# Five score banks for part of the scores, products cut in two, and a new written order, in clustered attention followed by a SoLU block

## The chip, the cores and the metric

The kernel runs on one core of one Trainium2 chip. The metric is the device time of one execution in microseconds (us). Matmuls run on TensorE (PE in the profile; PEld is its weight load), element-wise work on VectorE (DVE), ScalarE (ACT) and GpSimd (POOL); SyncE (SP) issues nearly all DMAs.

## The reference, cut to what matters

Clustered attention, then a SoLU feed-forward block with a layer norm. With B = 4, H = 8, S = 768, D = 64 and 16 clusters:

```
q_assign = argmax over c of <q_n, c_n>        # the same for k_assign
mask     = q_assign[:, :, :, None] == k_assign[:, :, None, :]
scores   = where(mask, q k^T / sqrt(D), -1e9)
x        = softmax(scores) @ v                # heads side by side: 3072 tokens x 512
h        = x @ w_in                           # 512 -> 1024
solu     = h * softmax(h)
out      = layernorm(solu) * g_ln @ w_out     # 1024 -> 512
```

## The kernel before, in words

*The attention.* Work goes by 16 pairs of heads (batch b, pair p). For each pair q and k are loaded (`ld`), turned so that features lie on partitions (batch 0: on TensorE through the region `hreg`, `tp`, and copied out, `xa`, L405; the others: on VectorE, `xt`, L419), multiplied by the centroids on TensorE (`cl`, L450, into the bank `csc`), turned back (`tb`, L471), reduced to a maximum per token (`mx`, L484), compared with it (`oh`, L489) and turned again (`ot`, L495). q and k are cast to bf16 into the tile `qk` (`ca`, L443 to L447) and the one-hot rows are placed beneath them (`pl`, L507, L512 or L514), with a zero fill (`bl`, L523), so that one matmul gives score plus cluster match. v is loaded (`lv`) and cast (`cv`, L532).

*Scores.* 294 score banks follow one another: 24 of 384 columns (the first pair), then 270 of 512. `S` (L593) writes a bank on TensorE, `E` (L599) is its exponential on ScalarE, `V` (L616) multiplies it by the values, `N` (L628, L641) divides a group of heads by its row sums on VectorE into x. Groups are numbered in order; groups 0 and 1 belong to the first pair, and a unit of the later ones has three banks. The scores take turns in a ring of three PSUM banks (`ps_s`); three more banks are `hreg`, one holds the values' sums (`ps_o`), one is shared by `cl`, y and small turns (`ps_m`).

*The feed-forward part.* It goes by 24 blocks f of 128 tokens. x is transposed by DMA, for two blocks at a time in the first three batches (`tx`, L671; the last block on TensorE); `h` (L702, four parts of two matmuls) fills two of hreg's three banks, even blocks the banks 0 and 1, odd ones 1 and 2; `hm` (L708) is the maximum, `ex` (L714) the exponential, `u` (L721) the product; u is transposed (`tu`, L726 by DMA; the last two blocks on TensorE, `ptu`); `bn` and `ag` (L732, L736) are the statistics, `at` and `al` (L742 to L751) the scale on GpSimd; `y` (L768, four parts) multiplies by w_out; `sc` (L786 or L788) scales, `ou` stores. w_out is prepared first: eight sums weighted by g (`su`, L568, L571), their mean over rows by a matmul (`me`, L576, into bank 2 of hreg), and eight centred rows (`ce`, L579).

*What sets the order.* Every step is registered by `add` with its engine, a cost, the steps that it needs, and others that it comes after. The tables `ORDER` list for each engine the kinds of steps in the order in which that engine issues them, written out by hand or by a planner outside of the program; the n-th step of a kind that was registered for an engine is the n-th of that kind in the table. `AWAY` gives single steps to another engine than their own. Each engine works through its queue in order, and waits where an operand or a bank isn't ready. `uses` (L230) tells which banks of `hreg` an instruction touches, so that those of other banks don't wait for it.

Of the kernel before, what the change touches and what calls it, by code (L numbers as in the profile page):

```python
# [10 lines left out]
F32 = mybir.dt.float32  # L11
# [11 lines left out]
class Weave:  # L23
# [6 lines left out]
        ld4 lv si ld3 lo lg ld3 lv ld lo ld3 lo lv ld4 lv lo li ld8 li3 tx ld4 tx ld2 lv3 tu ld7 tx  # L30
        tu ld8 tu ld3 ou ld lv3 tu ou ld ou ld9 tu ld9 ou tx tu ld tx ld5 lv ld7 tu lv tx ou tu ld7
        tu ou2 ld4 ou ld4 lv ld3 tu2 ld2 pl ou pl2 ld pl tx lv ld2 tu lv ou tx ou lv tu tx pl tu pl2
        ou pl tu2 ou tx tu ou tx3 ou tu2 tx ou tu ou2 tu2 ou6
    """
    ORDER["POOL"] = """
        ca3 cv2 pl bl ca2 pl2 ca2 pl2 ca2 pl z sg ca2 pl2 ca bl pl2 cv z cv ca pl ca2 cv4 pl2 bl pl
        ca3 z ca z2 wi4 ca2 pl4 ca cv3 pl2 at bl al pl2 bl ca cv at ca4 al ca at pl3 ca cv2 pl at al
        cv2 ca2 cv al cv at cv pl4 ca2 cv ca2 pl4 bl at al ca6 al pl3 ca at ca pl bl ca cv al pl ca
        cv pl3 at ca at bl ca5 al cv pl2 at bl pl2 cv al2 ca2 bl cv ca4 at2 al pl cv al pl2 ca pl ca
        pl bl po pl at ca pl ca cv2 pl bl ca2 at2 al2 at3 al2 at al at2 al2 at al2 at al2 at al  # L40
    """
    ORDER["PE"] = """
        wm tp2 cp tp cl tp fl4 cl fl tp2 S3 tp2 S cq S2 tp2 S3 cl V2 S V S2 tp2 gt S V3 S2 tp2 S3 cl
        S2 V2 S V S2 tp S2 tp S V S V S V S3 cl S2 V2 S2 V2 S3 V2 S2 V S V S2 cl S2 V2 S2 V2 S3 V2
        S2 V2 S3 V2 S2 V2 S2 me S2 V2 S2 V2 S2 cl S3 V4 S2 h S h S2 h2 S2 V2 S2 V2 S h2 V2 S2 h S V2
        S2 h2 S3 h V3 S2 y3 S y S2 V3 S2 h2 S3 V4 cl S h2 S2 y S V2 S2 y2 S2 y V S2 V h V S3 V h2 S
        V y V y S3 y V3 S2 V y S V S h S2 h2 S V S2 cl S3 V3 h y2 S V S2 y2 S2 V2 S cl V S3 V4 S h S
        V S2 h S h S2 cl S V2 S2 V2 y2 S2 V2 S V2 S2 y S y S2 V3 S V S2 h2 S h2 S2 h2 S V S V3 y2 S
        y S y h2 S3 V cl V h S2 cl S2 V3 h S3 V3 S h2 S2 y4 S2 V h V3 S3 V h V S2 h S h S V S h S y3
        S3 V4 h V S2 h S y S h S h V2 S cl V2 S3 cl V2 S3 y2 S2 y S V2 h S y V2 S3 V2 cl S2 h2 S3 V  # L50
        y4 S V3 S2 y S y S2 V3 S2 V S y2 S3 V3 S V S h2 S h S2 V h S V2 S h S2 V h S y3 V S3 V y h2
        S2 V2 S V S cl V2 S2 h V h S2 h S h V S2 h S y2 V3 S V2 S2 h S h S2 h V S2 V3 y h V S3 h y V
        S2 h2 V S2 h S V y2 h V2 S3 y2 S2 V h2 S2 V y2 S V2 S2 h y h S2 h2 S2 V3 y S2 V S h2 V3 S V
        h2 S3 y4 h2 S3 V h2 S V3 y2 h y2 V S3 h2 V h y4 h V2 h y4 h2 ptx y4 h2 y3 h2 y ptu2 y7 ptu2
        y5
    """
    ORDER["DVE"] = """
        cn cb tb mx oh ot pl3 tb mx oh ot xa2 cf ca2 bl tb mx oh gk ot N pl su xa su tb mx oh xa ot
        su xa N xt su pl tb mx N oh bl ot xt N su tb su pl N su2 N mx oh ot N xt2 ce2 N ce2 tb N ce3
        hm ce N u mx oh ot N hm xt bn2 ag u xt N bn hm bn xt ag tb u mx N bn oh ot xt2 hm bl N bn u  # L60
        ag xt bn2 ag sc hm N tb mx oh ot u bn2 N xt tb mx bl xt oh N hm ot tb N u mx ag N xt oh bn
        ot N bn xt hm xt ag u xt bn2 ag hm tb N u mx tb oh bn N ot hm xt bn u sc xt N ag mx hm oh
        bn2 u xt2 N hm ag ot tb xt tb N mx u mx xt oh bn ot bn tb N ag bn hm bn sc mx N cv xt oh2 N
        u ag ot N bn2 cv sc hm xt ag u N ot hm bn2 tb u N mx hm oh cv2 ot u N bn2 hm ag2 bl bn u N
        bn hm bn2 N u bn hm ag N u ag bn2 hm ag bn N u bn N hm u bn2 hm N ag bn ag2 u bn2 hm sc u N
        bn ag bn hm ag tx sc u bn2 hm tu2 ag u2 bn2 ag tu
    """
    ORDER["ACT"] = """
        wa xa4 ca3 xa2 E9 xa2 E3 xa2 E4 xa E59 ex E10 ex E8 sc E3 ex E10 sc E4 ex E12 ex E6 sc E13
        ex E13 sc E4 ex E4 sc E3 ex E10 ex E11 ex E6 sc E3 ex E10 sc E8 ex E19 ex E5 sc E4 ex E8 ex  # L70
        E9 ex E5 sc E2 ex E4 sc E4 ex E7 ex E2 sc E4 ex E2 sc E3 ex sc E3 ex sc ex sc ex sc tu sc3
        oz
# [3 lines left out]
        ca0.0.0.1.1 sc23.0 xa0.0.0.1 xa0.0.1.0 xa0.1.0.0 xa0.1.0.1 xa0.2.0.0 xa0.2.0.1 xa0.2.1.0  # L76
        xa0.2.1.1 xa0.3.0.0
    """.split(), "ACT"))
    AWAY.update(dict.fromkeys("""
        bl0.0.1 bl0.2 bl1.2 bl1.3 bl3.3 ca0.0.1.1.1 ca0.1.0.0 cv3.0.0 cv3.1.0 cv3.3.0 cv3.3.1  # L80
        pl0.0.0.1.1 pl0.1.1.0 pl0.2.0.1 pl0.3.0.0 sc10 sc17 sc19 sc2 sc6 sc9 tu22.0
    """.split(), "DVE"))
    AWAY.update(dict.fromkeys("""
        ca0.0.1.1.0 pl0.0.1.0.0 pl0.0.1.1.0 pl1.0.0.0 pl1.0.0.1 pl1.0.1.0 pl1.0.1.1 pl1.1.0.0
        pl1.1.0.1 pl1.1.1.0 pl1.1.1.1 pl1.2.0.0 pl1.2.0.1 pl1.2.1.0 pl1.2.1.1 pl1.3.0.0 pl1.3.0.1
        pl1.3.1.0 pl1.3.1.1 pl2.0.0.0 pl2.0.0.1 pl2.0.1.0 pl2.0.1.1 pl2.1.0.0 pl2.1.0.1 pl2.1.1.0
        pl2.1.1.1 pl2.2.0.0 pl2.2.0.1 pl2.2.1.0 pl2.2.1.1 pl2.3.0.0 pl2.3.0.1 pl2.3.1.0 pl2.3.1.1
        pl3.1.0.0 pl3.1.0.1 pl3.1.1.0 pl3.1.1.1 pl3.2.0.0 pl3.2.1.0 pl3.3.0.0 pl3.3.1.1
# [79 lines left out]
def kernel(  # L168
# [281 lines left out]
    def clusters(b, p, hf):  # L450
# [14 lines left out]
        asg[b, p, hf, "csc"] = csc  # L465
# [109 lines left out]
    def mean_w_out():  # L575
        uses(nc.tensor.matmul(hreg[:, 2, :], g_mean[:], w_sum[:]), 2)  # L576
# [8 lines left out]

    def scores(n, k):
        u = UNITS[n]
        b = u["b"]
        sps_[n, k] = ps_s.tile([P, 512], F32, name="sps", tag="sps")
        for h, kt, s0, w, c0 in u["banks"][k]:  # L590
            r = used(h % 2)
            keys = slice(kt * P, (kt + 1) * P) if by_token(b) else slice(kt, S, n_t)
            nc.tensor.matmul(sps_[n, k][:, c0:c0 + w], side(b, h // 2, 1, h % 2, keys)[r],  # L593
                             side(b, h // 2, 0, h % 2, slice(s0 * P, s0 * P + w))[r])

    def expo(n, k):
        w = wide(n, k)
        es[n, k] = ep.tile([P, 512], BF16, name="e")
        nc.scalar.activation(es[n, k][:, :w], sps_[n, k][:, :w], Act.Exp, scale=exp_scale,  # L599
                             bias=-exp_scale)  # L600
# [373 lines left out]
    for idx, (b, p) in enumerate(pairs):  # L974
        first = first_of(b, p)
        for hf in range(2) if halves_of(b, p) else (None,):
# [6 lines left out]
            add(f"cl{t}", "PE", (0.72 - 0.22 * hf if half else 1.45 if twelve(b, p) else 0.87), first - 9,  # L983
                (lambda e, b=b, p=p, hf=hf: clusters(b, p, hf)), kept + ["cf" if twelve(b, p) else "cb"], take="m")
# [267 lines left out]
```

## Time and profile before

| | |
|---|---|
| runs shown (us) | 230.77, 228.57, 228.95; median 228.95 |
| the profiled execution (us) | 228.39 |
| its span (us) | 226.4 |
| granted clock of TensorE | 0.999 |

The span is the time between the first and the last instruction on the engines. A row of a group gives line, engine, operation, output and inputs, shapes, count, then busy us and mean ns of one, then the idle time before them and what ended it. A row of the chain of waits or of the timeline gives the start in us, the duration, and what ran; "xN" is the number of instructions merged in it.

### The profile page before, as it was taken

The numbers are of one execution on the slowest core, as the hardware profiler recorded it, in microseconds if no ns is written. First come the engines' busy times: TensorE is split into PE (matmuls) and PEld (weight loads), VectorE is DVE, ScalarE is ACT, GpSimd is POOL, SyncE is SP. The second block draws the span as 40 slices with busy tenths as digits, with TensorE's granted clock in tenths as the row PEclk, the third lists the DMA queues.
The fourth block names the chain that finished last, engine by engine and source line by source line (L and its number), as shares of the span: only waits on it lengthen the run. The fifth ranks groups of instructions, "written<-read, shape, count | busy, mean of one in ns | idle before, by whom it ended". The sixth has DMA issues, their size and how long they took to land.

```text
span 226.4 us, 6687 instructions
## 1 busy us (share of the span) xinstructions
PE 218.4 (96%) x2460; PEld 148.7 (66%) x2460; DVE 200.4 (89%) x353; ACT 194.7 (86%) x378; POOL 132.9 (59%) x256
## 2 busy tenths in 40 slices
PE   7899988999999999999999999999999999999993
PEld 4566655666777767686577767687677677675452
DVE  3699999999999899999999989899899969798991
ACT  3689979999999999999889999899999999974352
POOL 4577799982498589387949742485908403223311
PEclk9999999999999999999999999999999999999999
DMA  6996988699998999999998949579924441476922
GB/s 154 343 353 163 258 226 120 256 157 252 149 172 147 248 229 181 146 166 163 185 232 144 215 101 210 126 161 210 243 59 110 97 116 26 61 150 181 186 86 106
DMA packets 123183, 39.00 MB, mean 172 GB/s; under 512 B 112008, under 2 KB 117904, under 8 KB 123152
## 3 DMA queue, kind: packets, MB, share of 16 engines
q1 hardware_dynamic: 122432, 38.06, 79.5%
q10 hardware_dynamic: 720, 0.52, 0.8%
q8 instruction: 19, 0.31, 0.6%
q14 instruction: 12, 0.10, 0.1%
HBM read 23.11 MB, written 6.29 MB: 130 GB/s over the span
## 4 chain that ended last, share of the span: by engine, by line
PE 74%; DMA 8%; DVE 8%; SPq 7%; issue 1%; ACT 0%; DVEq 0%
PE sps L593 22%; PE hreg L702 18%; PE yps L768 17%; PE ops L616 13%; SPq L411 4%; PE csc L462 3%; DMA w_g<-in_moe_w_out_dram 3%; DMA w_st<-in_moe_w_in_dram 2%; DVE w_out_c L579 2%; DMA raw<-in_k_dram 2%; DVE xt L419 1%; SPq L564 1%; DMA raw<-in_q_dram 1%; PE hreg L768 1%; SPq L376 1%
## 5 line engine op out<-in xcount | busy, mean ns | idle before, releaser
L599 ACT ACTIVATE e<-sps 128x512 bf16<-128x512 f32 (+1 forms) x294 | 151.8, 595 | 11.9 <-PE sps L593 10.1
L593 PE MATMUL sps<-qk 96*128 96x256 bf16 (+5 forms) x636 | 93.3, 264 | 2.1 <-DVE qk L507 0.6
L593 PEld LDWEIGHTS <-qk 96*128 96x128 bf16 (+1 forms) x636 | 59.5, 121 | 27.1 <-issue 7.6
L616 PEld LDWEIGHTS <-e 128*128 128x128 bf16 x1152 | 49.7, 97 | 12.1 <-issue 3.1
L616 PE MATMUL ops<-v,e 128*128 128x65 bf16 x1152 | 54.2, 193 | 0.6 <-DVE x L641 0.5
L702 PE MATMUL hreg<-w_in_sb,xT 128*128 128x512 bf16 x192 | 52.9, 379 | 0.3 <-DVE w_out_c L579 0.3
L768 PE MATMUL yps<-w_out_c,uT 128*128 128x512 bf16 x184 | 47.4, 378 | 0.0
L514 POOL COPY qk<-oht 32x384 f32<-32x384 f32 (+1 forms) x45 | 22.2, 493 | 19.5 <-DVE oht L495 17.1
L721 DVE TENSOR_TENSOR u<-e_sb,hreg 128x1024 bf16<-128x1024 bf16 (+1 forms) x25 | 29.1, 1169 | 2.8 <-ACT e_sb L714 2.5
L708 DVE TENSOR_REDUCE nmax<-hreg 128x1 f32<-128x1024 f32 x24 | 29.3, 1219 | 2.6 <-PE hreg L702 2.0
L732 DVE BATCH_NORM_STATS2 bs<-u 128x6 f32<-128x512 bf16 x48 | 31.2, 674 | 0.2
L714 ACT ACTIVATE e_sb<-hreg,nmax 128x1024 bf16<-128x1024 f32 x24 | 26.9, 1120 | 3.0 <-DVE nmax L708 2.9
L445 POOL CAST qk<-xt 64x768 bf16<-64x768 f32 (+1 forms) x32 | 26.5, 829 | 4.7 <-ACT xt L405 3.3
L447 POOL TENSOR_SCALAR qk<-xt 64x768 bf16<-64x768 f32 (+1 forms) x31 | 26.8, 864 | 2.2 <-DVE xt L405 0.2
L768 PEld LDWEIGHTS <-uT 128*128 128x128 bf16 x200 | 18.3, 97 | 14.2 <-ACT uT L698 0.5
L702 PEld LDWEIGHTS <-xT 128*128 128x128 bf16 x192 | 17.1, 97 | 10.0 <-DVE w_out_c L579 0.6
L419 DVE STREAM_TRANSPOSE xt<-raw 128x768 f32<-128x768 f32 x24 | 22.8, 958 | 0.0
L742 POOL TENSOR_SCALAR es<-esum 128x1 f32<-128x1 f32 x24 | 5.8, 246 | 27.1 <-ACT e_sb L714 26.5
L748 POOL TENSOR_SCALAR esq<-es,mv 128x1 f32<-128x1 f32 x24 | 8.3, 344 | 21.3 <-DVE mv L736 21.1
L641 DVE TENSOR_TENSOR x<-ops,den 128x256 bf16<-128x256 f32 (+1 forms) x39 | 19.0, 486 | 1.3
L532 POOL CAST v<-vf 128x384 bf16<-128x384 f32 x28 | 14.2, 522 | 5.9 <-DMA vf<-in_v_dram 4.5
L786 ACT ACTIVATE y<-yps,alpha 128x512 f32<-128x512 f32 x17 | 11.7, 690 | 6.6 <-PE yps L768 5.8
(79 smaller groups left out, 178.3 us busy)
## 6 DMA issues: line engine op xcount, KB each, us to landing
vf<-in_v_dram SPq DMA_DIRECT2D x16, 384.0 KB, 4.4
out_dram<-y SPq DMA_DIRECT2D x23, 256.0 KB, 2.7
raw<-in_q_dram SPq DMA_DIRECT2D x50, 96.0 KB, 3.1
raw<-in_k_dram SPq DMA_DIRECT2D x50, 96.0 KB, 3.2
w_g<-in_moe_w_out_dram SPq DMA_DIRECT2D x4, 512.0 KB, 7.2
w_st<-in_moe_w_in_dram SPq DMA_DIRECT2D x4, 512.0 KB, 5.3
raw<-in_q_dram SPq DMA_DIRECT2D x3, 384.0 KB, 6.6
raw<-in_k_dram SPq DMA_DIRECT2D x3, 384.0 KB, 7.0
```

Of the source, the lines that this page charges most:

```text
L419: nc.vector.transpose(xt[:], raws[b, p, i][:].rearrange("p j c -> p (j c)"))
L445: VEC[e].tensor_copy(dst, src)
L447: VEC[e].tensor_scalar(dst, src, scalar1=inv_C, scalar2=1.0, op0=Alu.mult, op1=Alu.mult)
L593: nc.tensor.matmul(sps_[n, k][:, c0:c0 + w], side(b, h // 2, 1, h % 2, keys)[r], side(b, h // 2, 0, h % 2, slice(s0 * P, s0 * P + w))[r])
L599: nc.scalar.activation(es[n, k][:, :w], sps_[n, k][:, :w], Act.Exp, scale=exp_scale, bias=-exp_scale)
L616: nc.tensor.matmul(opss[g][:, s, :VW], es[n, k][:, c0:c0 + P], v1[slot(b, h // 2)][:, h % 2, kt, :VW], start=(kt == 0), stop=(kt == n_t - 1))
L702: uses(nc.tensor.matmul(hreg[:, at(f, f2)[1], :], xTs[f][:, dc, :], w_in_sb[:, dc, f2 * FF2:(f2 + 1) * FF2], start=(dc == 0), stop=(dc == ...
L708: uses(nc.vector.tensor_reduce(ff[f, "nmax"][:], pair_of(f), axis=AXY, op=Alu.max, negate=True), *both(f))
L714: uses(nc.scalar.activation(ff[f, "e"][:], pair_of(f), Act.Exp, bias=ff[f, "nmax"][:], accum_out=ff[f, "esum"][:]), *both(f))
L721: uses(nc.vector.tensor_tensor(ff[f, "u"][:, r], ff[f, "e"][:, r], pair_of(f)[:, r], op=Alu.mult), *both(f)[r])
L732: nc.vector.bn_stats(ff[f, "bs"][:, f2, :], ff[f, "u"][:, f2, :])
L768: ins = nc.tensor.matmul(dst, ff[f, "uT"][:, at(f, f2)[0] * (n_fc // 2) + c, :], w_out_c[:, fc, cols], start=(fc == fcs[0] and part % 2 == ...
```

## The change

- *Five banks.* Of the scores numbered 24 to 65 (from 0), two in five are written into banks 0 and 1 of `hreg` in place of the ring's three. Their first use waits for the last token transpose in that bank, the next ones for the exponential that read the bank before, and the first h in these banks for the last such exponential. `aft` orders the scores as before.
- *Cuts.* For the pairs 1 to 3 of batch 0 the cluster product is issued as two steps, `ck` and `cl`, of four matmuls each that add up in one bank. The matmul for w_out's mean is issued as `me0` and `me1`, of 256 columns each. The centred rows need both.
- *Order.* `ORDER` is new for all five queues; in the planner that wrote it VectorE and GpSimd exclude each other.
- *Places.* `AWAY` is new. Steps by kind on each engine, where they differ:

| engine | before | after |
|---|---|---|
| VectorE | ca 2, cv 4, pl 6, bl 5, xa 5, sc 6, tu 3 | ca 7, cv 2, pl 4, bl 4, xa 6, sc 9, tu 1 |
| ScalarE | xa 11, ca 3, sc 19, tu 1 | xa 10, ca 8, sc 16, tu 3 |
| GpSimd | ca 63, cv 28, pl 54, bl 12 | ca 53, cv 30, pl 61, bl 13 |
| SP | pl 8 | pl 3 |

The diff without the tables:

```
     def clusters(b, p, hf, hh=None):
         lo, n = (0, HALF) if hf is None else (hf * HALF, QTR)
-        csc = ps_m.tile([P, HALF], F32, name="csc", tag="m")
+        if not hh:
+            asg[b, p, hf, "csc"] = ps_m.tile([P, HALF], F32, name="csc", tag="m")
+        csc = asg[b, p, hf, "csc"]
         if twelve(b, p):
-            for hh, c in ((hh, c) for hh in range(2) for c in range(4)):
+            for c in range(4):
...
-    def mean_w_out():
-        uses(nc.tensor.matmul(hreg[:, 2, :], g_mean[:], w_sum[:]), 2)
+    def mean_w_out(x):
+        cols = slice(x * FF2 // 2, (x + 1) * FF2 // 2)
+        uses(nc.tensor.matmul(hreg[:, 2, cols], g_mean[:], w_sum[:, cols]), 2)
...
+    spare_from, spare_to = 24, 66
+    slots = {BANKS[i]: (i - spare_from) % 5 for i in range(spare_from, spare_to)
+             if (i - spare_from) % 5 < 2}
...
     def scores(n, k):
...
-        sps_[n, k] = ps_s.tile([P, 512], F32, name="sps", tag="sps")
+        j = slots.get((n, k))
+        sps_[n, k] = (ps_s.tile([P, 512], F32, name="sps", tag="sps") if j is None else
+                      hreg[:, j, :])
...
+            if j is not None:
+                uses(ins, j)
...
-        if i >= ring_s:
-            nd.append("E{}.{}".format(*BANKS[i - ring_s]))
+        aft = ["S{}.{}".format(*BANKS[i - 1])] if i else []
+        if (n, k) in slots:
+            j = slots[n, k]
+            nd += [of_bank[j]] if j in of_bank else [
+                x for m, x in enumerate(ring_h[-3:], len(ring_h) - 3) if m % 3 == j]
+            aft += [] if j in of_bank else last_tp[-1:]
+            of_bank[j] = f"E{n}.{k}"
+        else:
+            nd += of_ring[-ring_s:][:1] if len(of_ring) >= ring_s else []
+            of_ring.append(f"E{n}.{k}")
...
                     else:
-                        nd += [x for j, x in enumerate(ring_h[-3:], len(ring_h) - 3)
-                               if j % 3 == bank]
+                        nd += [of_bank[bank]] if bank in of_bank else [
+                            x for j, x in enumerate(ring_h[-3:], len(ring_h) - 3) if j % 3 == bank]
```

The places of the steps on which the prediction rests, cut from the queues (names are kind, then block, unit or batch.pair, then part):

```
PE before   V13.0 V13.1 S15.0 S15.1 me S15.2 ... S18.2 S19.0 h0.0.0 S19.1 h0.0.1 S19.2 S20.0 h0.1.0 h0.1.1
PE after    V13.0 V13.1 S15.0 S15.1 S15.2 ... S18.2 h0.0.0 h0.0.1 h0.1.0 h0.1.1 S19.0 S19.1 S19.2 V17.0
DVE before  N5 mx1.0 oh1.0 ot1.0 N6 xt1.1.0 xt1.1.1 ce0 ce1 N7 ce2 ce3 tb1.1 N8 ce4 ce5 ce6 hm0 ce7 N9 u0
DVE after   N5 ce0 ce1 N6 ce2 oh1.0 ce3 N7 ce4 ce5 ot1.0 ce6 ce7 hm0 N8 tb1.1 u0
ACT before  E19.0 E19.1 E19.2 E20.0 E20.1 E20.2 ex0 E21.0
ACT after   E19.0 E19.1 ex0 E19.2 E20.0
PE's end before  h23.1.1 y20.3 ptu22 ptu22 y21 (4) y22.0 to y22.2 ptu23 ptu23 y22.3 y23 (4)
PE's end after   h23.1.1 ptu22 y20 (4) ptu22 y21 (4) y22.0 y22.1 ptu23 y22.2 y22.3 ptu23 y23 (4)
DVE's end before hm23 tu22 tu22 ag22 u23.0 u23.1
DVE's end after  hm23 bn22.1 ag21 ag22 sc20 u23.0 u23.1
```

More of the change, by code (lines that the diff above doesn't have):

```diff
@@ L41 @@
+        ca2 cv pl cv at al ca pl ca at2 ca3 pl3 bl pl2 cv at al2 at al at al po al at3 al4 at2 al2
+        at al
     """
     ORDER["PE"] = """
[L43 to L46, printed above, removed]
@@ L73 @@
+        E7 ex E11 ex E5 sc E ex E7 ex E6 ex E5 sc E2 ex sc E5 ex E2 sc E ex sc ex sc ex tu2 sc tu
+        sc3 oz
     """
@@ L1209 @@
             [f"lo{fc // 2}"] + ([f"su{fc - 1}"] if fc else ["gk"]))
-    add("me", "PE", 0.9, 36, lambda e: mean_w_out(), [f"su{n_fc - 1}", "sg"] + [
+    for x in range(2):
+        add(f"me{x}", "PE", 0.45, 36 + x, (lambda e, x=x: mean_w_out(x)),
+            ["me0"] * x + [f"su{n_fc - 1}", "sg"] + [
         x for j, x in enumerate(ring_h[-3:], len(ring_h) - 3) if j % 3 == 2], last_tp[-1:])
```

109 lines of the change are left out of this document (59 added, 50 removed).

## The prediction

> **What bounds the kernel now.** I read the page first (span, busy shares), then busy time by stretch, then the chain of waits, then the single instructions where the chain changes engine.
>
> ```profile
> span 226.4 us, 6687 instructions
> PE 218.4 (96%) x2460; PEld 148.7 (66%) x2460; DVE 200.4 (89%) x353; ACT 194.7 (86%) x378; POOL 132.9 (59%) x256
> ```
>
> Four engines are nearly full, so shares do not name the limit. By stretch (length; then PE, PEld, DVE, ACT, POOL busy; clock; DMA):
>
> ```profile
> 24.00:36.00 12.00, 10.77 (x139) 7.01 (x138) 11.65 (x22) 10.21 (x22) 10.34 (x19) 1.00 0.91 207
> 36.00:49.00 13.00, 12.11 (x182) 8.74 (x180) 12.71 (x24) 12.51 (x25) 12.43 (x17) 1.00 0.87 184
> 54.00:204.00 150.00, 150.00 (x1754) 106.91 (x1753) 137.83 (x233) 141.37 (x272) 87.37 (x164) 1.00 0.82 158
> ```
>
> From 54 to 204 TensorE has no idle time; VectorE has 12.2 us of it and ScalarE 8.6. Before 49 it is VectorE that is full (24.4 of 25 us). The chain of waits says the same, VectorE until 53.7, then TensorE until the last block's tail:
>
> ```profile
> 43.99 1.81 DVE xt L419 x2
> 49.97 1.97 DVE w_out_c L579 x3
> 53.08 0.67 DVE w_out_c L579
> 53.79 1.04 PE hreg L702 x4
> ...
> 215.11 0.86 PE hreg L702 x4
> 215.98 0.43 PE yps L768 x2
> ...
> 218.51 1.28 DVE u L721 x2
> ...
> 221.58 1.50 PE hreg L768 x12
> ```
>
> So the time is: when the feed-forward work starts to fill TensorE (h of block 0), plus the TensorE work then left, plus holes in it, plus the tail. The first of these is a chain through one normalisation (group 6, N6), its transpose by DMA and the first h:
>
> ```profile
> 43.45 0.14 DVE L628 RECIPROCAL den<-ops 128x4 f32<-128x4 f32 x1
> 44.08 1.34 SPq L671 DMA_TRANSPOSE xT<-x  x1
> 48.95 0.59 PE L702 MATMUL hreg<-w_in_sb,xT 128*128 128x512 bf16 x2
> 53.79 1.04 PE L702 MATMUL hreg<-w_in_sb,xT 128*128 128x512 bf16 x4 [0.34 <-DVE w_out_c L579]
> ```
>
> N6 starts at 43.45, the transpose is issued as it ends, and h starts 5.5 us after N6's start. The 0.34 is TensorE waiting for the last centred row of w_out, queued behind block 0's maximum.
>
> **The change part by part.** No matmul, exponential or normalisation comes or goes. Three cluster products and w_out's mean are cut in two at the same columns and passes, which I cost at nothing: the cut only lets other matmuls between. If a cut cost a drain of its own it would be four of them, in a stretch where TensorE idles anyway. What moves is order, and who does the small work.
>
> *Five banks.* ScalarE's exponentials before 49 us waited for scores here:
>
> ```profile
> 16.77 1.25 ACT L599 ACTIVATE e<-sps 128x384 bf16<-128x384 f32 x3 [0.67 <-PE ops L616]
> 22.08 5.85 ACT L599 ACTIVATE e<-sps 128x384 bf16<-128x384 f32 x13 [0.41 <-PE sps L593]
> 28.91 3.54 ACT L599 ACTIVATE e<-sps 128x512 bf16<-128x512 f32 x7 [0.98 <-PE sps L593]
> 32.74 0.60 ACT L599 ACTIVATE e<-sps 128x512 bf16<-128x512 f32 x1 [0.29 <-PE sps L593]
> 33.69 2.07 ACT L599 ACTIVATE e<-sps 128x512 bf16<-128x512 f32 x4 [0.35 <-PE sps L593]
> 38.67 8.74 ACT L599 ACTIVATE e<-sps 128x512 bf16<-128x512 f32 x17 [0.19 <-PE sps L593]
> ```
>
> That is 2.9 us. With five banks TensorE can be five scores ahead, and the 0.98 stood behind a whole cluster product, now halved with four scores between. I take 2.3 of the 2.9 as saved; the bounds are 0 (the scores' own operands are late) and 2.9. N6 needs the exponential of bank 53, which is the sixth of the last row: 38.67 + 5 x 8.74 / 17 + 0.5 = 41.7.
>
> *ScalarE's new casts.* Ahead of bank 53 its queue gets five casts more and one copy less. Three are half-size and stand before the first exponential, where they fill a wait for TensorE; two are of full size.
>
> ```profile
> L443 ACT ACTIVATE qk<-xt 64x384 bf16<-64x384 f32 x3 | 1.5, 517 | 0.0
> L405 ACT COPY xt<-hreg 128x384 f32<-128x384 f32 x11 | 5.2, 507 | 3.0 <-PE hreg L391 3.0
> ```
>
> A full one is not in the trace: between 0.52 (no growth) and 1.03 (double), I take 0.85, since an instruction has a fixed part. So +1.7 (1.0 to 2.1; up to 2.7 with the half ones unhidden). Bank 53: 41.7 + 1.7 - 2.3 = 41.1. Its values on TensorE add about 0.6, so N6 cannot start before 41.7.
>
> *VectorE up to N6.* In the order texts, ahead of N6 it loses one one-hot compare, one of its transposes and three full-size placements (now GpSimd's), and gains two input transposes, two centred rows and one copy:
>
> ```profile
> L489 DVE TENSOR_TENSOR oh<-cst,mx 128x384 bf16<-128x384 f32 x15 | 11.8, 790 | 0.2
> L495 DVE STREAM_TRANSPOSE oht<-oh 128x384 bf16<-128x384 bf16 x15 | 8.5, 565 | 0.2
> L507 DVE COPY qk<-oht 32x384 f32<-32x384 f32 x3 | 2.2, 747 | 0.1
> L419 DVE STREAM_TRANSPOSE xt<-raw 128x768 f32<-128x768 f32 x24 | 22.8, 958 | 0.0
> L579 DVE SCALAR_TENSOR_TENSOR w_out_c<-w_g,g_ln,hreg 128x512 bf16<-128x512 f32 x8 | 5.6, 736 | 0.0
> L405 DVE COPY xt<-hreg 128x384 f32<-128x384 f32 x5 | 2.6, 539 | 0.0
> ```
>
> Away: 0.79 + 0.57 + 3 x 0.75 = 3.6. Added: 2 x 0.96 + 2 x 0.74 + 0.54 = 3.9. The small rest (a half cast and two fills go, a half placement and a value cast come) I leave at -0.3. Net nothing: by these means N6 stays where it was, and only shorter instructions move it. The trace shows that they can be shorter, where GpSimd was busy beside them:
>
> ```profile
> 14.85 1.08 DVE L445 CAST qk<-xt 64x768 bf16<-64x768 f32 x1
> 13.79 1.73 POOL L447 TENSOR_SCALAR qk<-xt 64x768 bf16<-64x768 f32 x2 [0.19 <-DVE xt L405]
> 17.48 1.21 DVE L489 TENSOR_TENSOR oh<-cst,mx 128x384 bf16<-128x384 f32 x1
> 56.07 0.56 DVE L489 TENSOR_TENSOR oh<-cst,mx 128x384 bf16<-128x384 f32 x1
> L571 DVE SCALAR_TENSOR_TENSOR w_sum<-w_g,g_ln,w_sum 128x512 f32<-128x512 f32 x7 | 5.9, 837 | 0.0
> 28.45 0.71 DVE L571 SCALAR_TENSOR_TENSOR w_sum<-w_g,g_ln,w_sum 128x512 f32<-128x512 f32 x1
> ```
>
> The cast ends at 15.93, 0.41 after GpSimd's pair ends at 15.52: up to 0.67 of it was waiting. Three compares ahead of N6 could save 3 x (0.79 - 0.56) = 0.7 to 3 x (1.21 - 0.56) = 1.9, I take 1.4; seven sums 7 x (0.84 - 0.71) = 0.9. Together 3.0. Nothing in the program keeps the two engines apart; only the planned order does, and GpSimd still does most of its old work here. I take half, 1.6 (0 to 3.0): N6 at 43.45 - 1.6 = 41.85, just behind ScalarE's 41.7. The transpose's 5.5 us stay, so h starts at 47.35: **-1.6** (bounds: -1.75 to +2.0 by ScalarE, -3.0 to 0 by VectorE).
>
> The Trainium skill ("SBUF — State Buffer", section "Who interferes with whom") states that a VectorE copy or cast in a two-port mode, and one with two SBUF inputs against a GpSimd read, exclude GpSimd for a whole instruction, and that issue order decides who blocks. The cast's end at 15.93 agrees. By that rule an order that never lets them meet would save the whole 3.0, which is the second rival below and its 226.0; a plan that drifts by half an instruction would save nothing and be the first.
>
> *TensorE's queue at h.* One score bank and two groups of values that stood ahead of the first h now follow it. In the chain of waits they cost
>
> ```profile
> 67.96 0.44 PE sps L593 x4
> 204.62 0.19 PE ops L616 x6
> ```
>
> so half of 0.44 for a bank and 0.19 for a group: 0.22 + 0.38 = **+0.6**, since less is done when the full stretch begins.
>
> *Holes behind h.* The centred rows now all precede block 0's maximum, so the 0.34 goes. But the first exponential of the feed-forward part now stands four banks earlier in ScalarE's queue, four banks' exponentials wait behind it, and the score that needs one of them for its ring place stops TensorE. I take a hole as large as the one that goes, the nearest row for such a stop. Together **0** (-0.3 if there is none, +1.0 if it is four times as long).
>
> *GpSimd and SP.* SP loses five placement DMAs late in the kernel, GpSimd takes them as copies and gives up ten casts. GpSimd's 87 busy of 150 covers that; uncovered, each copy would hold a score for its own length. Loads before the first transpose are the same set in another order: nothing.
>
> *Tail.* Behind the last h TensorE holds twelve y parts of earlier blocks, before it was nine: the last h ends 3 x 0.43 = 1.3 earlier. Between VectorE's last maximum and its last product one output scaling comes (0.75, row under the rivals; a statistics and an aggregate that come and two copies that go I hold equal). It lies partly beside the last exponential, and the last y parts meet a copy that is later by as much, so I let all of it and a little count: -1.3 + 0.8 = **-0.5** (-1.3 if the exponential covers it, 0.2 if two such waits show).
>
> Sum: -1.6 + 0.6 + 0 - 0.5 = -1.5. The profiled execution took 228.39 (span 226.4 and 2.0 around it); the median of the runs shown is 228.95, 0.56 higher. 228.39 - 1.5 = **226.9**.
>
> **Rivals.** *They collide as before* (for it: no wait enforces the plan; against: the full placements, which collide, leave VectorE). N6 stays: 0 + 0.6 - 0.5 = 228.5.
>
> *Both early limits give all.* ScalarE waits nowhere (bank 53 at 40.5, N6 at 41.1 or, with shorter casts, 40.9) and VectorE saves 3.0: -2.5 + 0.6 - 0.5, so 226.0. For it: the 0.98 has a plain cause that goes. Against: both must be perfect at once.
>
> *ScalarE's casts are not paid back*: no wait saved, bank 53 at 43.4, N6 at 44.1: +0.65 + 0.6 - 0.5 = 229.1. Against it stand the two banks.
>
> *VectorE becomes the bound behind h* (the slower side). Behind its first maximum it gets six full casts and three output scalings, and loses three value casts and two uT copies.
>
> ```profile
> L788 DVE TENSOR_SCALAR y<-yps,alpha 128x512 f32<-128x512 f32 x6 | 4.5, 746 | 1.3 <-issue 0.8 <-PE yps L768 0.6
> ```
>
> A cast costs 0.41 to 1.08 (above), so +4.7 to +8.7, less about 1.8: 3 to 7, I take 5. Its 12.2 us of idle time in 54 to 204 should take that in; where that idle time is all waiting for TensorE's results in order, it does not, and TensorE waits instead. It decides once less than 5 of the 12.2 can be used; then all of it shows: 5 - 1.6 + 0.6 - 0.5 = +3.5, so 231.9.
>
> **How the numbers follow.** Chances: forecast 0.40 (own range 225.7 to 228.1), collide as before 0.18, all given 0.16, casts unpaid 0.09, VectorE the bound 0.17. A measurement of this kernel tells about 1% from no change, 2.3 us: faster means under 226.1, slower over 230.7. Faster: nearly all of "all given" (0.15) and a quarter of the forecast (0.10), 0.25. Slower: VectorE the bound, and 0.03 from holes elsewhere, 0.20. Same: 0.55. The range leaves out half of the cases under 226 and most of the VectorE case: 225.5 to 230.8.
>
> **What would show it.** N6 (the reciprocal before the first transposing DMA) at about 41.9 and the first h at 47.4; ScalarE's waits for scores before 49 under 1 us; the mean compare nearer 0.6 than 0.79; no hole over 0.5 us in TensorE from 54 to 204; the last h 1.3 us nearer the front of the tail. The forecast is wrong if TensorE shows idle time behind h, if N6 is not earlier than 43, or if the compare keeps its 0.79.

## The result, and the profile after

The changed kernel takes 225.36 us (median of 4 runs, 224.93 to 226.01) against 228.76 us for the kernel before on the same chip (4 runs, 228.23 to 230.77). The ratio is 0.985, with a 95% interval of 0.981 to 0.989: 3.4 us less, where 1.5 us were forecast. The forecast of 226.9 is 1.5 too high, and the time lies just under the range's low end of 225.5. Here and below, times and ratios leave out a few executions, of the kernel before and of three variants, that were over 1.5% above the fastest of their kernel at a lower granted clock.

The profiled execution is the slowest of the four, 226.01, with a span of 223.9. The page of the changed kernel:

```profile
span 223.9 us, 6670 instructions
PE 216.5 (97%) x2432; PEld 149.6 (67%) x2462; DVE 198.3 (89%) x355; ACT 195.3 (87%) x381; POOL 130.4 (58%) x256
```

Busy time by stretch (length; PE, PEld, DVE, ACT, POOL; clock; DMA):

```profile
24.00:36.00 12.00, 11.46 (x171) 7.61 (x167) 11.73 (x23) 11.76 (x26) 10.22 (x17) 1.00 0.89 190
36.00:49.00 13.00, 12.88 (x172) 9.39 (x170) 12.86 (x23) 12.51 (x27) 7.74 (x12) 1.00 0.80 230
54.00:202.00 148.00, 146.39 (x1713) 106.00 (x1737) 138.34 (x234) 138.62 (x267) 87.97 (x168) 1.00 0.81 158
```

Shares of the whole span say next to nothing, PE went from 96% to 97%. The stretch 24 to 49 tells it: TensorE is busy 24.34 of 25 us, before 22.88. ScalarE went from 22.7 to 24.3. VectorE is as full as it was. (The stretch ends at 49, which is 0.05 us behind the first h before and 2.8 us behind it after.) The chain of waits has moved from VectorE to TensorE. From 44.0 to 53.7 it was transposes, w_out rows and VectorE's normalisations; now it is TensorE without a break from 34.4 to 50.2, of which this is a part:

```profile
39.62 0.43 PE hreg L579 x2
40.06 0.22 PE hreg L602 x2
40.28 0.23 PE sps L602 x2
40.53 0.92 PE ops L629 x24
41.45 0.44 PE sps L602 x4
41.89 0.44 PE hreg L602 x4
42.33 0.78 PE csc L465 x8
```

(hreg L602 are scores in the two added banks.) The single instructions of the head, to be held against those at 43.45, 44.08 and 48.95 before:

```profile
41.62 0.18 DVE L641 RECIPROCAL den<-ops 128x4 f32<-128x4 f32 x1
42.28 2.31 SPq L684 DMA_TRANSPOSE xT<-x  x1
46.19 0.61 PE L715 MATMUL hreg<-w_in_sb,xT 128*128 128x512 bf16 x2
```

N6 starts 1.83 us earlier and h follows it after 4.57 us in place of 5.50: h is 2.76 us earlier. From there on little differs. The hole in TensorE behind h is 0.40 us (for a score whose bank waits for ScalarE), where there was one of 0.34. From 54 to 202 there is one of 0.20, at 171.3, for a normalisation on VectorE, where there was none; what the first column lacks besides are 26 steps of about 0.05, which I put down to missing records (2432 matmuls are in this trace, 2460 in that of before). From the start of the first h to the end of the last it takes 166.5 us, before 167.0; from there to the end of the span 11.2, before 10.4.

ScalarE's waits from 10 to 49, in the view of waits (total, times, longest), before (two rows) and after (one):

```profile
ACT e L599 <- PE sps L593: 2.8, 8, 1.0
ACT e L599 <- PE ops L616: 0.7, 1, 0.7
...
ACT e L610 <- PE sps L602: 0.9, 4, 0.3
```

Of VectorE's groups ahead of N6, three as they were and four as they are now:

```profile
L489 DVE TENSOR_TENSOR oh<-cst,mx 128x384 bf16<-128x384 f32 x4 | 4.5, 1120 | 0.1
L514 DVE COPY qk<-oht 32x192 f32<-32x192 f32 x3 | 1.3, 418 | 0.1
L568 DVE TENSOR_SCALAR w_sum<-w_g,g_ln 128x512 f32<-128x512 f32 x1 | 0.9, 946 | 0.0
...
L573 DVE SCALAR_TENSOR_TENSOR w_sum<-w_g,g_ln,w_sum 128x512 f32<-128x512 f32 x7 | 6.3, 900 | 0.1
L491 DVE TENSOR_TENSOR oh<-cst,mx 128x384 bf16<-128x384 f32 x3 | 1.7, 553 | 0.1
L446 DVE CAST qk<-xt 64x768 bf16<-64x768 f32 x1 | 0.7, 673 | 0.0
L570 DVE TENSOR_SCALAR w_sum<-w_g,g_ln 128x512 f32<-128x512 f32 x1 | 0.4, 443 | 0.0
```

The three compares have a mean of 0.553, against 1.120 for the four in the same place before. Over the whole kernel the mean went from 0.790 to 0.642. The sums did not get shorter (0.900, before 0.837).

```profile
L491 DVE TENSOR_TENSOR oh<-cst,mx 128x384 bf16<-128x384 f32 x15 | 9.5, 642 | 0.2
L516 DVE COPY qk<-oht 32x192 f32<-32x192 f32 x4 | 1.2, 312 | 0.1
```

The first row is that of the whole kernel. The second, of the time ahead of N6 again, is half-size placements, which had a mean of 0.418 there before.

### The profile page after: what moved, and what is told of

The parts are those of the page before. It is cut to its first block, busy times and chain, and to the rows that moved or that the text cites. A ratio compares the mean times of both kernels' runs of the same rounds, so it can differ in the third digit from the quotient of the medians.

```text
span 223.9 us, 6670 instructions
## 1 busy us (share of the span) xinstructions
PE 216.5 (97%) x2432; PEld 149.6 (67%) x2462; DVE 198.3 (89%) x355; ACT 195.3 (87%) x381; POOL 130.4 (58%) x256
## 4 chain that ended last, share of the span: by engine, by line
PE 85%; DVE 10%; issue 2%; ACT 2%; POOL 0%; DVEq 0%; ACTq 0%
PE sps L602 25%; PE hreg L715 17%; PE yps L781 16%; PE ops L629 14%; PE csc L465 4%; PE hreg L396 2%; PE hreg L392 2%; PE csc L460 1%; DVE w_sum L573 1%; PE idle_p L829 1%; DVE xt L420 1%; DVE u L734 1%; DVE oh L491 1%; PE hreg L602 1%; DVE oht L497 1%
## 5 line engine op out<-in xcount | busy, mean ns | idle before, releaser
L610 ACT ACTIVATE e<-sps 128x512 bf16<-128x512 f32 (+1 forms) x276 | 143.9, 605 | 9.4 <-PE sps L602 8.6
L602 PE MATMUL sps<-qk 96*128 96x256 bf16 (+5 forms) x600 | 86.9, 264 | 0.6 <-ACT e L610 0.4
L602 PEld LDWEIGHTS <-qk 96*128 96x128 bf16 (+1 forms) x636 | 60.1, 121 | 27.4 <-issue 9.0
L629 PE MATMUL ops<-v,e 128*128 128x65 bf16 x1152 | 52.6, 194 | 0.6 <-DVE x L654 0.5
L715 PE MATMUL hreg<-w_in_sb,xT 128*128 128x512 bf16 x180 | 49.3, 379 | 0.7
L781 PE MATMUL yps<-w_out_c,uT 128*128 128x512 bf16 x166 | 45.8, 379 | 0.7
L516 POOL COPY qk<-oht 32x384 f32<-32x384 f32 (+1 forms) x49 | 24.5, 501 | 17.7 <-DVE oht L497 11.9
L446 POOL CAST qk<-xt 64x768 bf16<-64x768 f32 (+1 forms) x27 | 22.3, 825 | 5.4 <-ACT xt L406 2.5
L448 POOL TENSOR_SCALAR qk<-xt 64x768 bf16<-64x768 f32 x26 | 22.6, 871 | 1.9 <-DVE xt L406 0.2
L534 POOL CAST v<-vf 128x384 bf16<-128x384 f32 x30 | 15.9, 547 | 2.0 <-PE yps L781 1.1
L764 POOL TENSOR_TENSOR alpha<-esq,halves 128x1 f32<-128x1 f32 x24 | 13.4, 560 | 2.0
```

What stands on the lines that cost most here:

```text
L448: VEC[e].tensor_scalar(dst, src, scalar1=inv_C, scalar2=1.0, op0=Alu.mult, op1=Alu.mult)
L516: ins = VEC[e].tensor_copy(dst.bitcast(F32), src.bitcast(F32).unsqueeze(1) .to_broadcast([NB, 2, n // 2]))
L602: ins = nc.tensor.matmul(sps_[n, k][:, c0:c0 + w], side(b, h // 2, 1, h % 2, keys)[r], side(b, h // 2, 0, h % 2, slice(s0 * P, s0 * P + w) ...
L610: ins = nc.scalar.activation(es[n, k][:, :w], sps_[n, k][:, :w], Act.Exp, scale=exp_scale, bias=-exp_scale)
L629: nc.tensor.matmul(opss[g][:, s, :VW], es[n, k][:, c0:c0 + P], v1[slot(b, h // 2)][:, h % 2, kt, :VW], start=(kt == 0), stop=(kt == n_t - 1))
L715: uses(nc.tensor.matmul(hreg[:, at(f, f2)[1], :], xTs[f][:, dc, :], w_in_sb[:, dc, f2 * FF2:(f2 + 1) * FF2], start=(dc == 0), stop=(dc == ...
```

## The experiments

Each kernel ran on a chip beside the kernel before; ratios are to that, with 95% intervals. The changed kernel, run again beside e1_three, e3_whole and e4_tail, took 225.83 us and has 0.986 (0.981 to 0.991); the others ran on other chips, and are set against it by their ratios.

**Runs of the same kernels.** Three profiles more, without an edit, because TensorE's first rows differed between the two traces.

> The changed kernel again, to part what the change does from what differs between runs. In its first profile TensorE's transposes at 3.85 took 2.83 us where the kernel before has 1.72, and the transposing DMA before the first h took 0.9 us less than there. Theory: the slow first 10 us are a run's own, the earlier landing is the kernel's (TensorE, SP and the loads ahead are where the plan put them). Then the transposes take about 1.7 us, the reciprocal before the first transposing DMA is at 40.8 to 41.4, h follows 4.3 to 4.8 us later, and the span is near 223. Rival: the slow start comes with the new order and the landing is chance; then 2.8 us again, the reciprocal at 41.6 again, and h anywhere from 4 to 6 us behind it.

> The kernel before again, for one profile more. In five profiles of the changed kernel and its variants TensorE's transposes of the first 10 us went over from 0.42 us each to 0.27 between 4.7 and 7.2 us after the start; in the one of the kernel before at 4.3. Theory: that moment is a run's own, so in another run of the kernel before it can fall later, and then all that follows is later by up to 1.1 us with the same distances. Rival: it belongs to the new order, and the kernel before has it at 4.3 again.

> The changed kernel a third time, one profile. In its two profiles TensorE came to its full rate at 7.2 us, in seven profiles of other kernels between 4.1 and 7.2. Theory: that moment is a run's own; if it falls early this time, the first exponential starts at about 11.0 in place of 12.05 and all behind it is earlier by that, the span 222.8 to 223.2, except that h may wait for its transposing DMA by up to 0.5 us. Rival: the changed kernel always starts slowly; then 7.2 and 223.9 again.

The transposes at 3.85 in the first profile of the changed kernel, in that of the kernel before, and then in a second one of the kernel before and in two variants whose first 10 us are the changed kernel's own instructions (e1_three and e6_place):

```profile
3.85 2.83 PE L392 MATMUL hreg<-ident_f,raw 128*64 128x128 f32 x24
```

```profile
3.84 1.72 PE L391 MATMUL hreg<-ident_f,raw 128*64 128x128 f32 x24
```

```profile
3.84 1.87 PE L391 MATMUL hreg<-ident_f,raw 128*64 128x128 f32 x24
```

```profile
3.84 1.94 PE L392 MATMUL hreg<-ident_f,raw 128*64 128x128 f32 x24
```

```profile
3.85 1.57 PE L392 MATMUL hreg<-ident_f,raw 128*64 128x128 f32 x24
```

Single transposes take 0.42 us up to some moment and 0.27 behind it; two of them start every 0.21 us before it and every 0.11 behind it, so the rate doubles. (The granted clock in the profile's rows is 1.00 throughout and does not show this.) The first transpose of 0.27 us starts at 4.3 and 4.7 in the kernel before, at 7.2, 7.2 and 6.9 in the changed one, and at 4.1 to 7.3 in the variants. I had expected it early in the second profile of the changed kernel and in the third; both were late (spans 223.9 and 223.7). That the changed kernel always starts slowly is still excluded: e1_three and e6_place run the same instructions up to 10 us and have it early, and e2_before_five, in the orders of the kernel before, has it late, at 6.2. The eleven executions of the changed kernel have spans from 222.8 to 223.9, as wide as this moment would make them. So it is a run's own. It moves the first exponential (12.05 in the changed kernel, 11.34 before, 10.95 in the second profile of before) and with it all that follows. Counted from the first exponential, and so without it, N6 is at 29.57, 29.61 and 29.46 us in the changed kernel and at 32.11 and 32.10 before; h at 34.14, 34.12 and 34.18 against 37.61 and 37.60; the end of the span at 211.8 (211.82, 211.80, 211.88) against 215.1 (215.04, 215.19). **That is 3.3 us, the median's 3.4, and it hid in the one pair of profiles behind a start that was 0.7 us later.**

The Trainium skill ("TensorE: Matmul & The Clock Gate", section "What's actually happening") has the rule for the moment: the array runs at half rate until a free-running window of about 3.4 us has been busy, so the change of rate depends on where in the window the first matmul falls. The trace agrees in kind (the rate doubles 2.9 to 6.2 us after the first matmul at 1.17); the spread that the page gives, 0.5 us either way, is smaller than the 4.1 to 7.3 here.

**Order and banks apart.** Two edits: the changed kernel with three score banks, and the kernel before, in its own orders, with five (its first bank in the added place is 29, since its order has the last input transpose behind bank 24).

```diff
e1_three:        -    spare_from, spare_to = 24, 66
                 +    spare_from, spare_to = 24, 24
e2_before_five:  + scores, expo and the needs of S and E as in the change,
                 +    spare_from, spare_to = 29, 66
```

> The changed kernel with three score banks throughout, all orders as they are. Theory: the two extra banks are what took ScalarE's waits for scores away. Without them these waits before 49 us go from 0.9 to 2.5 or more, bank 53's exponential ends at least 1.5 us later, the reciprocal before the first transposing DMA is at 42.8 or later, and the time is 1 to 2.5 us over the changed kernel's. Rival: the new order alone keeps the scores ahead; then the waits stay under 1.5 and the time within 0.5 of the changed kernel's.

> The kernel before, in its own orders, with two more score banks from bank 29 to 65. Theory: VectorE, full in its order, holds the reciprocal before the first transposing DMA at 43.4 there, so the banks alone shorten ScalarE's waits (from 3.4 to about 2 before bank 53) and the time by 0 to 0.8 us. Rival: the banks are the change, the order is only what carries them; then that reciprocal comes 1.5 us or more earlier and the time falls by 1.5 to 3 us.

New orders with three banks: 228.69, ratio 1.000 (0.997 to 1.003). Old orders with five: 228.74, ratio 0.999 (0.996 to 1.003). Each alone brings nothing measurable, together they bring 1.5%. Both first theories have the direction of the time right and a size wrong. Without the banks e1_three is 2.9 us over the changed kernel, where 1 to 2.5 were named, and its waits before 49 come to 2.0, where 2.5 or more were. In e2_before_five the banks do not shorten ScalarE's waits at all: 3.3 before bank 53, as in the kernel before, where about 2 was expected. The stretches show why the time stays. e1_three, then e2_before_five:

```profile
24.00:36.00 12.00, 10.94 (x145) 7.10 (x146) 11.10 (x19) 11.14 (x23) 9.31 (x16) 1.00 0.88 196
36.00:49.00 13.00, 12.05 (x164) 8.49 (x161) 11.12 (x22) 11.94 (x24) 5.90 (x7) 1.00 0.78 205
```

```profile
24.00:36.00 12.00, 9.93 (x135) 6.54 (x134) 11.62 (x22) 10.31 (x22) 10.36 (x18) 1.00 0.96 208
36.00:49.00 13.00, 11.68 (x182) 8.72 (x181) 12.71 (x23) 12.67 (x26) 12.38 (x18) 1.00 0.64 151
```

The reader compares VectorE's column, the third of the busy ones. With the new orders and three banks it is busy 22.22 of 25 us: the orders did give VectorE room, but nothing is ready for it sooner, TensorE (22.99) and ScalarE (23.08) still step from bank to bank. With the old orders and five banks VectorE is at 24.33, and TensorE idles more than before (21.61): scores run ahead and then all wait for VectorE. Only with both are TensorE, VectorE and ScalarE full at once. N6 counted from the first exponential is at 32.1 in both, as in the kernel before. On that way, from the first exponential to N6, VectorE is busy 31.0 of 32.1 us before and in e2_before_five, and nothing holds it up for longer than 0.15 us; in e1_three it is busy 28.1 and waits three times for values on TensorE (0.64, 0.42 and 0.74 us); in the changed kernel it is busy 27.4 of 29.6.

TensorE's rows hold part of the gain where idle time does not show it. From the start of one score matmul to the start of the next instruction, with idle time over 0.06 us taken out, the 113 scores between the first exponential and h take 16.8 us before, the 111 in the changed kernel 15.1, the 111 of e1_three 16.6 and the 113 of e2_before_five 15.7. A short wait between two matmuls lies under the modelled end of the first, and counts as busy. So of the 3.47 us by which h follows the first exponential sooner, 1.6 is idle time that TensorE no longer has, 1.7 the scores (some 0.2 of it the bank that now stands behind h), 0.4 two groups of values that now stand behind h too, and 0.2 other matmuls go the other way.

**The cut of the cluster products.**

```diff
-  add(f"ck{t}", ... clusters(b, p, hf, 0))   add(f"cl{t}", ... clusters(b, p, hf, 1))
+  add(f"ck{t}", ... [clusters(b, p, hf, x) for x in range(2)])   add(f"cl{t}", ... None)
```

> The changed kernel with the three cluster products whole again, at the place of their first halves. Theory of the prediction: the cut matters only through the scores that it lets between, so ScalarE loses 0.3 to 1 us once more around 30 us, and the time rises by 0 to 0.6 us. Rival: with five banks ScalarE has enough scores ahead, and the whole product is even better, as VectorE gets its result one score bank earlier; then no wait comes and the time is the same or up to 0.5 less.

227.04, ratio 0.993 (0.990 to 0.996): 1.2 us more than the changed kernel by the medians, 1.6 by the ratios, and more than either expectation. The waits come back not around 30 us alone but at the first product, and N6 follows, at 31.3 from the first exponential, 1.8 later than in the changed kernel; TensorE, ScalarE (two rows) and VectorE:

```profile
14.31 1.50 PE L460 MATMUL csc<-xt,w_out_c 128*32 128x384 f32 x16
...
16.12 1.25 ACT L610 ACTIVATE e<-sps 128x384 bf16<-128x384 f32 x3 [0.86 <-PE sps L602]
27.93 1.72 ACT L610 ACTIVATE e<-sps 128x512 bf16<-128x512 f32 x3 [0.34 <-PE sps L602]
43.45 0.17 DVE L641 RECIPROCAL den<-ops 128x4 f32<-128x4 f32 x1
```

In the changed kernel the wait at the first place is 0.21: three score matmuls stand between the halves of the product, which take 0.85 us each. There are still only three banks at 16 us, so a whole product of 1.5 us leaves ScalarE without a score.

**What VectorE and ScalarE carry.** Three placements back from GpSimd to VectorE (e6_place), two full-size casts back from ScalarE to GpSimd (e5_casts), each with its places in the orders.

```diff
e6_place:  +  AWAY["DVE"]: pl0.1.1.0 pl0.2.0.1 pl0.3.0.0
e5_casts:  -  AWAY["ACT"]: ca0.1.1.0 ca0.2.0.1
```

> The changed kernel with three full-size placements moved from GpSimd back to VectorE, as in the kernel before. Theory of the prediction: VectorE is full ahead of the reciprocal before the first transposing DMA, each costs it 0.75 us or less, so the reciprocal comes 1 to 2.2 us later and the time rises by 0.8 to 2 us. Rival: in the changed kernel VectorE is no longer the bound there (ScalarE is, 0.2 us away), its slack takes the placements up and they reach the scores earlier than from GpSimd; then the time changes by less than 0.5 us.

> The changed kernel with the two full-size casts that ScalarE took on given back to GpSimd, at the places in its queue that the kernel before gives them. Theory of the prediction: ScalarE loses 0.85 us by each, so its first exponential to bank 53's takes 28.7 - 1.7 = 27.0 us; but TensorE has only 1 us of idle time left in the whole of the changed kernel, so the time falls by 0 to 0.7 us. Rival: on GpSimd they come late for the scores or hold VectorE up; then ScalarE waits for scores by as much as it gains and the time rises by 0.5 to 2 us.

e6_place: 226.78, ratio 0.990 (0.987 to 0.994), about 1 us more than the changed kernel, at the low end of the theory's range (1.6 by its profile, from the first exponential to the end). The placements are shorter there than in the kernel before (0.747):

```profile
L509 DVE COPY qk<-oht 32x384 f32<-32x384 f32 x3 | 1.4, 465 | 0.1
```

3 x 0.465 = 1.4 us on VectorE, and N6 is 31.09 from the first exponential, 1.5 later. e5_casts: 225.77, ratio 0.987 (0.982 to 0.992), no measurable difference from the changed kernel. ScalarE gives up 1.7 us of casts and waits 1.5 us more before bank 53 (2.1 in place of 0.6), as the rival had it, and N6 hardly moves (29.77 from the first exponential). Its one profile is longer all the same: 213.1 us from the first exponential to the end, where the changed kernel has 211.8, with h 0.8 later, 0.5 of it a wait for the transposing DMA. The run began early (first exponential at 11.09), so its time alone does not show that. Whether the casts are worth anything to the time stays open.

**VectorE beside GpSimd, by itself.** Instructions on scratch tiles behind VectorE's last one in the kernel (cut and shortened here): a series of VectorE alone, then the same beside GpSimd's casts.

```diff
+ def series(): 6 compares; 6 casts 64x768; 6 sums; 6 transposes   (VectorE)
+ series()
+ for _ in range(24): nc.gpsimd.tensor_copy(b_pool[:D, :S], b_src[:D, :])
+ series()
```

> The changed kernel with a measurement behind its last instruction, whose time is no part of the kernel's: VectorE runs 6 compares, 6 casts (64x768), 6 sums and 6 transposes of the shapes in question on tiles of its own, first with GpSimd idle, then again beside 24 casts of 64x768 on GpSimd. Theory: what made compares (0.55 to 1.28 us), sums (0.63 to 1.19) and casts (0.41 to 1.08) of one shape differ in the traces is a GpSimd instruction running beside them. Then the first series shows about 0.55, 0.41, 0.63 to 0.71 and 0.57, each alike, and the second shows compares and casts of 0.8 to 1.3, sums of 0.8 to 1.2, and transposes unchanged or nearly. Rival: the long ones waited for something else (TensorE's or ScalarE's access, a semaphore); then both series are alike.

```profile
220.51 3.46 DVE L1265 TENSOR_TENSOR oh<-cst,mx 128x384 bf16<-128x384 f32 x6
223.89 3.48 DVE L1270 CAST qk<-xt 64x768 bf16<-64x768 f32 x6
227.29 4.67 DVE L1272 SCALAR_TENSOR_TENSOR w_sum<-w_g,g_ln,w_sum 128x512 f32<-128x512 f32 x6
231.88 3.64 DVE L1275 STREAM_TRANSPOSE cst<-xt 128x384 f32<-128x384 f32 x6
236.36 5.96 DVE L1265 TENSOR_TENSOR oh<-cst,mx 128x384 bf16<-128x384 f32 x6
236.58 25.99 POOL L1280 CAST qk<-xt 64x768 bf16<-64x768 f32 x24 [17.17 <-DVE xt L1278]
242.24 6.64 DVE L1270 CAST qk<-xt 64x768 bf16<-64x768 f32 x6
248.81 6.87 DVE L1272 SCALAR_TENSOR_TENSOR w_sum<-w_g,g_ln,w_sum 128x512 f32<-128x512 f32 x6
255.61 3.63 DVE L1275 STREAM_TRANSPOSE cst<-xt 128x384 f32<-128x384 f32 x6
```

Six compares go from 3.46 to 5.96 us, six casts from 3.48 to 6.64, six sums from 4.67 to 6.87; the transposes stay at 3.64. So an overlap with a GpSimd cast costs a compare 0.4, a cast 0.5 and a sum 0.4 us, and a transpose nothing: the theory holds, though a cast alone takes 0.58 here and not 0.41. They wait for each other: each compare and cast ends about 0.41 us after the GpSimd cast beside it, as the one at 15.93 did in the kernel before, and GpSimd's casts take 1.03 us beside compares and casts, 1.16 beside sums and 0.82 beside transposes. The rule that the prediction cited (the Trainium skill, "SBUF — State Buffer", section "Who interferes with whom") agrees for the compare, the cast and the sum; it does not name this transpose.

**TensorE's last instructions.**

```diff
-  ptx h2 y h2 y3 h2 y4 h2 ptu y4 ptu y6 ptu y2 ptu y4
+  ptx h2 y h2 y3 h2 y7 h2 y ptu2 y7 ptu2 y5
```

> The changed kernel with TensorE's last instructions (from the transposes for x on) in the order of the kernel before: three y parts fewer behind the last h. VectorE's scaling sc20 stays. Theory of the prediction: the last h ends 1.3 us later and is worth about 0.5 us of time net, so the time rises by 0.3 to 1.0 us. Rival: the tail is set by the chain of exponentials, products and copies behind the last h, and y parts are needed there to fill it; then the time is the same or less by up to 0.5.

227.41, ratio 0.993 (0.990 to 0.996): 1.6 us more than the changed kernel, above the expectation. The last h ends at 214.8 (212.7 in the changed kernel), and on its way TensorE waits for ScalarE to empty a bank of y:

```profile
212.51 1.46 PE L781 MATMUL yps<-w_out_c,uT 128*128 128x512 bf16 x6 [0.91 <-ACT y L799]
```

Three y parts (1.3 us) and this wait are the 2.2, and 0.8 comes back behind it. No such wait stands on the way to the last h in the kernel before, so it belongs to the mixture, the old TensorE order beside the new ones of ScalarE and VectorE, and 1.6 us is probably more than the old tail costs in its own kernel.

**The first transposing DMA.** Three loads moved ahead of it on SP, alone and with the casts of e5_casts.

```diff
-  li4 tx ld2 lv tx ld5 tu
+  li4 ld2 lv tx2 ld5 tu
```

> The changed kernel with three loads (two of q, one of v) moved on SP's queue from behind the first transposing DMA to ahead of it, where SP idles for 6 us; two transposing DMAs then follow each other. Theory: that DMA took 3.1 to 4.7 us in ten profiles as transfers that start beside it share its queues; with these gone it takes 3.1 to 3.6 and h comes up to 1 us earlier where the start was quick, but TensorE has little idle time left, so the time falls by 0.1 to 0.6 us. Rival: its length has another cause or h is not waited for; then the time is within 0.2 of the changed kernel's (225.4 to 225.8 on these chips).

> The last one and the casts given back to GpSimd together. With the casts on GpSimd the reciprocal before the first transposing DMA came at 40.9 and TensorE then waited 0.51 us for that DMA, which took 4.4 us. Theory: a DMA of 3.5 us turns that wait into time, 0.4 to 0.7 us less than the changed kernel. Rival: the two edits do not add, within 0.2 of the changed kernel.

Both miss. e8_loads has 226.89, ratio 0.989 (0.982 to 0.997), e9_loads_casts 227.94, ratio 0.996 (0.992 to 1.000): the second is slower than the changed kernel, and so is the first by its trace, with 214.2 us from the first exponential to the end of the span in place of 211.8:

```profile
41.88 4.85 SPq L684 DMA_TRANSPOSE xT<-x  x2
48.08 1.89 PE L715 MATMUL hreg<-w_in_sb,xT 128*128 128x512 bf16 x7 [2.33 <-DMA xT<-x]
```

The DMA that should have become shorter took 6.1 us to land (5.0 in e9_loads_casts), and TensorE stood for it for 2.33 us. It landed after 3.6 us in all three profiles of the changed kernel, and after 4.6 and 4.0 in the two of the kernel before. In the other variants with the changed kernel's order on SP it took 3.1 to 4.4 (4.2 in e1_three, 4.4 in e5_casts). So the order on SP alone does not set the length, and loads issued ahead of it did not make it shorter. What sets it stays open.

No variant was faster than the changed kernel.

## Why the prediction was wrong, step by step

*The steps that failed are those that make up the -1.6 for h.* Against the first exponential h came 3.5 us earlier: N6 by 2.5, and h by another 0.9 behind it. Two gains were mis-sized, and the path from N6 to h was wrong.

*VectorE's shorter instructions, "I take half, 1.6 (0 to 3.0)".* Mis-sized. Ahead of N6 the three full compares save 3 x (1.12 - 0.55) = 1.7, the two half ones 0.3, the cast 0.4, the first sum 0.5 and the half placements 4 x (0.418 - 0.312) = 0.4; the seven sums lose 0.4. That is 2.9, nearly the whole 3.0. That it comes so near is in part luck, as the parts are not those that I named: no gain came from the seven sums, which I had at 0.9, and more from compares and small copies. The mechanism, exclusion between VectorE and GpSimd, was right, and e7_lock shows it with the rest of the kernel gone. The net content of nothing nearly stands too: VectorE's rows up to N6 add up to 38.6 us before and 35.4 after, and of these 3.2 the shorter instructions leave 0.3. The placements that went to GpSimd are worth about 1 us of time by e6_place.

*"N6 ... just behind ScalarE's 41.7".* Also mis-sized. From its first exponential to the end of bank 53 ScalarE took 30.38 us and now takes 28.69: 1.7 less, where I had 2.3 - 1.7 = 0.6. My bounds by ScalarE, -1.75 to +2.0, were wrong as well: the terms beside them put N6 between 40.4 (41.7 + 1.0 - 2.9 + 0.6) and 45.0 (41.7 + 2.7 + 0.6), which is -3.0 to +1.6, and -1.75 is the middle value. On the clock of the kernel before's profile N6 came at 40.9 (11.34 + 29.57). The casts cost what I took (predicted 0.85):

```profile
16.68 0.84 ACT L444 ACTIVATE qk<-xt 64x768 bf16<-64x768 f32 x1
```

The waits fell by 2.7 (3.34 to 0.63 before bank 53), predicted 2.3. That leaves 1.7 - (2.7 - 1.7) = 0.7, which is ScalarE's other work on this way: without the casts it keeps the engine busy for 26.3 us, before 27.0 (the five copies 0.2 less, the rest in exponentials that overlap more).

*"The transpose's 5.5 us stay".* They became 4.57, 4.51 and 4.72, a further 0.9 that I had at nothing. The path was wrong: h did not wait for the transposing DMA. In the second profile of the kernel before it landed after 4.0 us, at 47.7, TensorE worked without idle time until h, 0.85 us later, and N6 to h was 5.50 again (SP's row, its landing, then TensorE's rows):

```profile
43.67 1.34 SPq L671 DMA_TRANSPOSE xT<-x  x1
DMA to landing us min/median/max: 4.0/4.0/4.0
48.10 0.60 PE L593 MATMUL sps<-qk 80*128 80x256 bf16 x4
48.55 0.60 PE L702 MATMUL hreg<-w_in_sb,xT 128*128 128x512 bf16 x2
```

In all five profiles of the two kernels the DMA has landed 0.2 to 0.9 us before h, and no row of h has an idle time before it. So h came when TensorE's own queue reached it. One bank and two groups less stand ahead of it, and these are the 0.6 that my next term counted as work left behind h; I had not let h come earlier by them, so that my sum holds the loss without the gain. The other 0.3 is not split further. e1_three agrees: with three banks TensorE gets to h 5.44 us behind N6, 0.58 after the landing. Only where the DMA landed late did h wait for it, in e5_casts (0.51), e9_loads_casts (1.22) and e8_loads (2.33).

*How I weighed them.* The rival "both early limits give all", 226.0, is what happened up to N6 (its 40.9 to 41.1), and I gave it 0.16 since "both must be perfect at once". The 0.9 behind N6 it lacks too. e1_three and e2_before_five show the flaw: the two limits are not independent chances. Each alone gains nothing as the other holds N6, and an order made for five banks frees both in one. Half of VectorE's gain was the mean of these two cases, 32.1 and 29.5 from the first exponential to N6, and describes neither.

*The cuts, costed at nothing.* Each cut of a cluster product costs TensorE 0.14 us (from start to start the three take 4.71 us cut and 4.29 whole, in e3_whole). Still e3_whole is 1.2 to 1.6 us slower, so the cut is a part of the gain, and the 0.98 that I saw at 28.9 was not the only place. What the cut of w_out's mean is worth by itself was not tested.

*TensorE's queue at h (+0.6), the hole (0), the tail (-0.5).* Right in sum: 0.25 more from the first h to the end, where 0.1 was predicted. From h to the last h it took 0.55 less (0.6 - 1.3 = -0.7 predicted), from there to the end 0.8 more, as predicted. The hole behind ex0 is 0.40, for 0.34 before.

*The starting point.* The sum was taken off the profiled execution, 228.39. Off the median of 228.76 the same -1.5 gives 227.3, so that the forecast misses by 1.5 us and not by 1.9 is luck.

*The rivals that did not come.* They do not collide as before: the compare's mean is 0.642, though the seven sums got longer. ScalarE's casts were paid back: bank 53 came 1.7 us sooner in spite of them. VectorE is no bound behind h: TensorE waits for it once from 54 to 202, for 0.20 us, and VectorE's busy time there rose by 2.5 us (135.9 to 138.3 of 148). GpSimd covers its new copies.

*What should show it.* N6 was to be near 41.9 (41.62), ScalarE's waits under 1 us (0.9), the compare nearer 0.6 (0.642), no hole over 0.5 (0.20): all as written. That N6 fits is luck: the run began 0.7 us later, and from the first exponential N6 came 2.5 us earlier, where 1.6 were forecast. The first h, 47.4 predicted, was at 46.19 even so.

## What to carry to other kernels

When two engines both hold up the same instruction, relieving one shows nothing in the time, and a forecast that takes half of a gain lies between the two cases: ask what happens when both go at once, and test each alone. Before a distance is called the DMA's, look whether the engine was idle until it landed: here TensorE never was, and its own queue set the time. Before two traces are compared instruction by instruction, look for a difference that has nothing to do with the change, here the moment at which TensorE came to its full rate, and count from an event behind it. A full TensorE share can still hold waits, if they are shorter than the modelled end of a matmul: the distance from start to start shows them.

## What the runs showed of the hardware

- A VectorE compare, cast or fp32 sum beside a GpSimd cast took 1.0, 1.1 and 1.15 us in place of 0.58, 0.58 and 0.78; a VectorE transpose stayed at 0.61. The GpSimd cast took 1.03 to 1.16 us beside the first three and 0.82 beside the transposes.
- TensorE doubled its rate (two fp32 transposes every 0.21 us, then every 0.11) between 4.1 and 7.3 us after the start, from run to run, with the same instructions; it moved the first exponential by up to 1.1 us.
- A product of sixteen matmuls, cut into two halves of eight, took TensorE 0.14 us more than whole.
- One transposing DMA of the same tile landed 3.1 to 6.1 us after its issue, in kernels that differ little around it.
